# First channel product of a token and channel mixer: four of twelve output tiles of blocks 2 to 5 by seven block products

## The chip, the cores and the metric

One core of one Trainium2 chip. The metric is device time in microseconds (us) of one execution; lower is better. TensorE (PE) does the matmuls and writes PSUM, which has eight banks of 128 partitions x 512 float32. VectorE (DVE) and ScalarE (ACT) work elementwise on SBUF and PSUM, GpSimd (POOL) and SyncE (SP) mostly issue DMAs. Each engine executes its own instructions in the order in which they were issued.

## What is computed

Eight batches of 3008 rows. First a gated attention, then an MLP mixer over tokens and one over channels, each with a residual:

```python
scores = (1.0 / S) * np.matmul(z, z.transpose(0, 2, 1))     # z: 8 x 3008 x 64
attn = np.maximum(scores, 0.0) ** 2
x = u * np.matmul(attn, v)                                  # u, v: 8 x 3008 x 256
...
xt = x.transpose(0, 2, 1)
h = np.maximum(xt @ w_tok1, 0.0) @ w_tok2                   # w_tok1: 3008 x 256
u = x + h.transpose(0, 2, 1)
h2 = np.maximum(u @ w_ch1, 0.0) @ w_ch2                     # w_ch1: 256 x 1536
return u + h2
```

The change concerns `u @ w_ch1` with its ReLU: 256 input channels (two tiles of 128) and 1536 output channels (twelve tiles of 128).

## The kernel before

**Tiles.** A batch's 3008 rows are cut into six blocks of up to 512 rows, q = 0 to 5 (the last has 448). Matmuls are in bfloat16 with float32 sums. PSUM is used as four pairs of two banks (`bank_pair`, L188); a pair is taken by `take_slot` (L940), which picks the one that comes free first, and is returned to the list `ring` with the time at which its reader will be done.

**AV phase.** For each block q the kernel makes scores (`score_run`, L448, line L465), their ReLU on ACT (L503, L491 for the triangle blocks), their square on DVE (L511, L542), and multiplies with v into two accumulators, each a pair of banks (`av_matmul`, L684, line L692; two matmuls of 64 rows run side by side). As the scores are symmetric, a block (q, g) with g > q is also turned by a DMA on SP for later use as (g, q) (`flip`, L558, line L562); it lies in one of the eleven "fl" buffers until then. At a block's end (`finish`, L804) ACT copies one half of an accumulator into a "cp" tile (L820), DVE adds the other half (L826, this frees the pair), and `gate` (L836, lines L846 and L851) multiplies with u into the block's tile `xT`, channels on partitions. This happens for each of the two channel halves, dh = 0 and 1; with dh = 0 the `xT` tile is allocated. "cp" tiles and the transposed `u_sb` tiles of `turn_u2` (L1129, line L1133) share three buffers with the tag "res".

**Mixer work.** It comes in rounds on PE, at the start of a batch's first AV block: first blocks 3 to 5 of the old batch, then the new batch's token mixer (`tok1` L1031, `tok2` L1105, whose result DVE adds to `xT` at L1114), then blocks 0 to 2 of the new batch. A block's channel mixer is:

- six pieces of `ch1` (L1149, line L1162), c2 = 0 to 5. A piece makes two of the twelve output tiles: four matmuls of 512 columns into one bank pair, and one ReLU of 128 x 1024 on ACT (L1201) into the tile `h2pre`.
- four sums of `h2pre` on DVE for each group d of four tiles (`make_sums`, L1227, lines L1241 to L1253) into "hsum", which lies in an "fl" buffer.
- seven products of twelve 128-column matmuls (`product`, L1272, line L1298): the second channel product is already done by seven block products instead of eight, on the sums of `mix_weights`. They go into two pairs, `xb` and `zb`, and DVE collects them (L1334) into "ro", also an "fl" buffer.

The order on PE within a block is written out by hand (end of `add_mixer`): `(0, 0, 1, 2, 0, 6, 5, 0, 7, 3, 0, 4)`, where 1 to 7 are the products of block q and 0 is the next `ch1` piece of block q + 1. So five of the six pieces of block q + 1 are made among the products of block q, and the sixth stands in front of its own products. Block 3's pieces are so made in one round and its products in the next; the sums of its first tiles are put off (`late_sums`) until the end of the AV phase between.

**Planner.** All instructions are placed by host code that keeps a model of the clock: every piece of work has an estimated cost, times at which its inputs will be ready (`Done`), and limits on live buffers (`ROOM`, for example nine `xT`, eleven "fl"). `push` queues an operation for ACT, DVE or SP; the one with the earliest start goes next. Mixer pieces go in the order of their list; AV work goes where no piece is ready. The semaphores for real dependences follow from the tiles.

Of the kernel before, what the change touches and what calls it, by code (L numbers as in the profile page):

```python
# [7 lines left out]

# [5 lines left out]
P = 128  # L14
# [43 lines left out]
def kernel(  # L58
# [42 lines left out]
    w_ch2_sb = consts.tile([P, CHT, D], BF16)  # L101
    w_mix_sb = consts.tile([P, 4, CHT // 2, P], BF16)
    w_sum_sb = consts.tile([P, 3, KT // 2, P], BF16)
    ident = consts.tile([P, P], BF16)

    zs = consts.tile([P, KT + 2, d_qk], BF16)
# [697 lines left out]
    def finish(blk, dh, end):  # L804


        W, acc = blk.W, blk.acc[dh]
        summed = Done()
        guess[blk.home[dh]] = end + 1.7
        ring.append((summed, blk.home[dh]))  # L810

        def load(e):
            return max(free[e], end) + sum(op.busy for op in waiting[e])

        on_act = blk.b > 0 or load("act") + 0.46 < load("dve") + 0.67

        def copy(t):
            cp = sb.tile([P, QW], F32, tag="res", name="cp", bufs=3)
            if on_act:
                nc.scalar.copy(cp[:, :W], acc[:, 1, :W])  # L820
            else:
                nc.vector.tensor_copy(cp[:, :W], acc[:, 1, :W])
            push("dve", t, 0.66, 0.78, lambda t: add(cp, t), first=1, done=summed)

        def add(cp, t):
            nc.vector.tensor_add(cp[:, :W], acc[:, 0, :W], cp[:, :W])  # L826
            push("dve", t, 0.58, 0.7, lambda t: gate(blk, dh, cp, t), first=1,
                 room=(lambda: (blk.b, blk.q) in uTs and has_room(("xT",))) if dh == 0
                 else lambda: (blk.b, blk.q) in xTs)
# [144 lines left out]
    def mix_weights(t):  # L974
# [19 lines left out]

        step(t)

    BORROW = 3
    VERY_LAST = (B - 1, NQ - 1, CHT // 2 - 1)
    ORDER_LAST = ((1, 2, 6, 5, 7, 0, 3, 4), (1, 2, 6, 5, 0, 7, 3, 0, 4))

    def add_mixer(b):
# [97 lines left out]
        def tok2(q, end):  # L1099
            slot, _ = take_slot()  # L1100
            W = widths[q]
            h = bank_pair(slot, "h_ps")
            for dh in range(DT):
                for th in range(2):
                    nc.tensor.matmul(  # L1105
                        h[:, dh, :W], st["a"][:, th, dh * P:(dh + 1) * P],
                        w_tok2_sb[:, th, q * QW:q * QW + W], start=(th == 0), stop=(th == 1))

            def add(t):

                xT = xTs[b, q]
                n = full_tiles[q]
                to = xT[:, :, :n * P].rearrange("p h (t s) -> p h t s", t=n)
                nc.vector.tensor_add(  # L1114
                    to, to, h[:, :, :n * P].rearrange("p h (s t) -> p h t s", t=n))
# [7 lines left out]
                u_done[q].t = t  # L1123
                st["turned", q] = push("sp", t, 1.25, 5.5, lambda t: turn_u2(q, t), first=1,
                                       room=lambda: has_room(("us",)) and (
                                           q <= HALF or goal[0] > (b, 1 + HALF)))
            ring.append((push("dve", end + 0.21, 1.12, 1.25, add, first=2), slot))

        def turn_u2(q, t):  # L1129
            live["us"] += 1  # L1130
            turned_back[b] += 1
            us = sb.tile([P, DT, QW // P, P], BF16, tag="res", name="u_sb", bufs=3)
            nc.sync.dma_start_transpose(  # L1133
                out=us.rearrange("p h t d -> p (h t) d"),
                in_=xTs[b, q].rearrange("p h s -> p (h s)"))
            st["u", q] = us
            release("xT", xT_uses[q])
            for waits in st.pop(("waits", q), []):
                waits(t)

        def with_u(q, ready, fn):

# [6 lines left out]
        def ch1(q, c2, borrowed, end):  # L1149
# [63 lines left out]
                              done=h2_done[q, c2]), slots[0]))  # L1213
            if c2 == CHT // 2 - 1:
                release("xT", xT_uses[q])

        def pairs_of(q):

            return 2 if q < NQ - 1 else 1

        def tiles_of(q, d, r, m):

            n = pairs_of(q)
            return st["h2", q, d].rearrange("p (j r) w -> p j r w", r=2)[
                :, :, r, :2 * n * P].rearrange("p j (i m s) -> p j i m s", m=2, s=P)[:, :, :, m, :]

# [82 lines left out]
        def collect(q, k, end):  # L1309
# [18 lines left out]
            def add(t):  # L1328
                if k == 1:
                    home, n_home = take_home(q)  # L1330
                    st["res", q] = sb.tile([P, QW // P, D], F32, tag=home, name="ro",
                                           bufs=n_home)
                m, h = blocks_of[k]
                nc.vector.tensor_add(  # L1334
                    res(m, h), source, us(m, h) if opening else res(m, h))
                recent[0] = st["res", q][:, 0, :1]
                over[q] -= 1
                if not over[q]:
                    nc.sync.dma_start(
                        out=rows_of(out[b], q)[:, :2 * n, :], in_=st["res", q][:, :2 * n, :])  # L1340
                    free["sp"] = max(free["sp"], t) + 0.4
                    release(home_of(q), [1], t + 4.0)
                    release("us", us_uses[q])

            ready = end + 0.21
            done = taken[q, k]
# [36 lines left out]
        def ch2(q, half, i, end):  # L1383
# [23 lines left out]
            def residual(t):  # L1407
# [28 lines left out]
                        nc.sync.dma_start(out=to, in_=res[r, j, :])  # L1436
                free["sp"] = max(free["sp"], t) + 0.4
                if last:
                    release("us", us_uses[q])
# [11 lines left out]
        def add_ch1(q, c2, by):  # L1451
# [2 lines left out]
                               lambda end: ch1(q, c2, by < q, end),  # L1454
                               room=("h2",) if c2 % 2 == 0 else (),
                               key=(b, 2 + by)))

        def halves(q):

# [43 lines left out]
        for q in range(NQ):  # L1503
            while added[q] < CHT // 2:
                add_next(q, q)
            rest = [(half, i) for half in halves(q) for i in range(pieces_of(q, half))]
            if fast(q):
                us_uses[q][0] += bool(rest)
                h2_uses[q] += bool(rest)
                for k in ORDER_LAST[b % 2] if q == NQ - 1 else (0, 0, 1, 2, 0, 6, 5, 0, 7, 3, 0, 4):  # L1510
                    if k:
# [216 lines left out]
    at_group(NQ * NG + (HALF - 1) * NG + 2,  # L1728
             lambda: push("dve", pe[0], 0.36, 0.5, mix_weights, first=-1))

    def ask_w_tok2(c):
        load_w_tok2(c)
# [189 lines left out]
```

## Time and profile before

| | |
|---|---|
| median of 3 runs | 1113.19 us (1113.01 to 1119.92) |
| profiled execution, first to last instruction (span) | 1110.5 us |
| granted TensorE clock in the profiled execution | 1.000 |
| PE busy | 1105.7 us, 11073 matmuls |
| DVE busy | 782.5 us |
| ACT busy | 669.4 us |
| first channel product (L1162) in the chain that ended last | 22% of the span |
| AV (L692) in that chain | 42% |
| second channel product (L1298) in that chain | 19% (xb 11%, zb 8%) |

The profiled execution's time is known as its span; the runs' times include what lies around it. In a timeline row the columns are start (us from the span's start), duration of the merged group, engine, line, operation, output <- input, shape, count, and in brackets the idle time before it with what ended it. Matmul durations overlap, so the pace of PE is read from start to start. In a row of groups, behind the count: busy us in total, mean ns of one, idle time of the engine before them and what ended it. In a row of windows: from:to, length, then busy time and count of PE, PE's weight loads (PEld), DVE, ACT and POOL, then granted clock, DMA share and GB/s. In a row of waits: who waited for whom, us in total, times, longest. A round of mixer work begins at 198.2, 335.5, 472.2, 607.7, 744.4, 880.0 and 1014.3 us.

### The profile page before, as it was taken

To read this page: it belongs to the slowest core of one execution; us is meant where nothing else is said; L and a number is where in the kernel's file an instruction comes from. 1 tells how busy PE (TensorE), PEld (TensorE's weight loads), DVE (VectorE), ACT (ScalarE), POOL (GpSimd) and SP (SyncE) were. 2 spreads that over 40 slices of the span, in tenths; PEclk is the share of its full clock that TensorE was granted. 3 is DMA by queue.
4 is the path that set the end of the run, shared out by engine and by line. 5 is a ranking of instruction groups with operands and counts; after the bars stand their busy time and mean duration, and the time that the engine had idled before them with its cause. 6 is when DMAs were issued, how large, how long until landed. Compare 5 with 4: busy or idle time off the path is not lost.

```text
span 1110.5 us, 27244 instructions
## 1 busy us (share of the span) xinstructions
PE 1105.7 (100%) x11073; PEld 683.8 (62%) x11073; DVE 782.5 (70%) x1888; ACT 669.4 (60%) x843; POOL 164.3 (15%) x382
## 2 busy tenths in 40 slices
PE   9999999999999999999999999999999999999998
PEld 3444575766557665576556865557655676556676
DVE  6889865975758857588566885578756777556775
ACT  7999555645854567545665456653666536743454
POOL 5320110221003110032100311003210120000100
PEclk9999999999999999999999999999999999999999
DMA  9999947796977969779697797967979678693222
GB/s 177 155 194 164 192 98 143 141 174 134 191 133 141 180 148 174 133 147 203 135 183 119 131 214 139 172 123 152 202 154 170 111 148 182 127 164 93 67 58 96
DMA packets 465725, 165.54 MB, mean 149 GB/s; under 512 B 433024, under 2 KB 448960, under 8 KB 465600
## 3 DMA queue, kind: packets, MB, share of 16 engines
q1 hardware_dynamic: 436208, 131.11, 58.6%
q0 software_dynamic: 28880, 32.32, 21.2%
q8 instruction: 86, 1.41, 0.5%
q10 hardware_dynamic: 512, 0.38, 0.1%
q14 instruction: 39, 0.32, 0.1%
HBM read 65.40 MB, written 24.64 MB: 81 GB/s over the span
## 4 chain that ended last, share of the span: by engine, by line
PE 99%; DMA 1%; issue 0%; POOL 0%; DVE 0%; POOLq 0%
PE acc L692 42%; PE hp L1162 22%; PE xb L1298 11%; PE zb L1298 8%; PE sc L465 6%; PE h_ps L1105 4%; PE a_ps L1031 3%; PE op L1398 2%; PE first_acc L609 1%; DMA v_sb<-in_v_dram 1%; PE zp L184 0%; PE up L1700 0%; DVE res L1433 0%; POOL ident masks.py:199 0%; POOL ident masks.py:197 0%
## 5 line engine op out<-in xcount | busy, mean ns | idle before, releaser
L1201 ACT ACTIVATE h2pre<-hp 128x1024 bf16<-128x1024 f32 (+1 forms) x287 | 278.5, 1008 | 204.0 <-PE hp L1162 171.5
L692 PEld LDWEIGHTS <-v_sb 64*128 64x128 bf16 x4418 | 246.3, 94 | 210.9
L692 PE MATMUL acc<-at,v_sb 64*128 64x512 bf16 (+1 forms) x2738 | 340.9, 375 | 0.0
L503 ACT ACTIVATE at<-sc 128x1024 bf16<-128x1024 f32 (+1 forms) x290 | 286.6, 1027 | 62.5 <-PE sc L465 54.8
L1162 PE MATMUL hp<-xT,w_ch_sb 128*128 128x512 bf16 (+1 forms) x1152 | 274.7, 375 | 0.0
L511 DVE TENSOR_TENSOR at<-at 128x1024 bf16<-128x1024 bf16 (+1 forms) x290 | 198.2, 687 | 103.8 <-ACT at L503 99.9
L692 PE MATMUL acc<-fl,v_sb 64*128 64x512 bf16 (+1 forms) x1680 | 192.5, 367 | 0.0
L1162 PEld LDWEIGHTS <-w_ch_sb 128*128 128x128 bf16 x1152 | 105.6, 98 | 98.1 <-issue 3.0
L1298 PEld LDWEIGHTS <-hsum 128*128 128x128 bf16 x2088 | 124.4, 98 | 18.2 <-issue 0.3
L465 PE MATMUL sc<-zT 64*128 64x512 bf16 (+1 forms) x732 | 131.8, 359 | 0.2 <-ACT zT L1750 0.2
L1298 PEld LDWEIGHTS <-h2pre 128*128 128x128 bf16 x1566 | 95.5, 98 | 20.1
L820 ACT COPY cp<-acc 128x512 f32<-128x512 f32 (+1 forms) x94 | 54.9, 584 | 77.8 <-PE acc L692 66.8
L826 DVE TENSOR_TENSOR cp<-acc,cp 128x512 f32<-128x512 f32 (+1 forms) x94 | 63.5, 676 | 50.7 <-ACT cp L820 50.1
L1241 DVE TENSOR_TENSOR hsum<-h2pre 128x512 bf16<-128x512 bf16 (+1 forms) x141 | 56.1, 402 | 40.7 <-ACT h2pre L1201 39.4
L491 ACT ACTIVATE at<-sc 128x512 bf16<-128x512 f32 (+3 forms) x152 | 56.2, 447 | 41.5 <-PE sc L465 41.0
L1298 PE MATMUL xb<-w_mix_sb,hsum 128*128 128x128 bf16 x1044 | 73.7, 219 | 0.0
L1334 DVE TENSOR_TENSOR ro<-xb,u_sb 128x256 f32<-128x256 f32 (+1 forms) x141 | 56.5, 401 | 22.5 <-PE xb L1298 20.5
L542 DVE TENSOR_TENSOR at<-at 128x512 bf16<-128x512 bf16 (+3 forms) x152 | 41.5, 321 | 38.2 <-ACT at L491 38.2
L465 PEld LDWEIGHTS <-zT 64*128 64x128 bf16 x732 | 42.8, 94 | 41.2 <-issue 3.6
L124 POOL CAST mark<-at 128x1 f32<-128x1 bf16 x24 | 8.2, 342 | 372.5 <-DVE at L511 372.5
L846 DVE TENSOR_TENSOR xT<-cp,uT 128x512 bf16<-128x512 f32 (+1 forms) x94 | 62.5, 665 | 0.9
L1253 DVE TENSOR_TENSOR hsum<-h2pre,hsum 128x512 bf16<-128x512 bf16 (+1 forms) x141 | 56.6, 401 | 2.3
(89 smaller groups left out, 968.4 us busy)
## 6 DMA issues: line engine op xcount, KB each, us to landing
out_dram<-ro SPq DMA_DIRECT2D x40, 512.0 KB, 3.0
v_sb<-in_v_dram POOLq DMA_DIRECT2D x40, 256.0 KB, 4.6
ur<-in_u_dram POOLq DMA_DIRECT2D x40, 256.0 KB, 4.9
w_tok_sb<-in_moe_w_tok_dram POOLq DMA_DIRECT2D x10, 256.0 KB, 10.7
zs<-in_z_dram POOLq DMA_DIRECT2D x35, 64.0 KB, 3.8
at<-at SPq DMA_TRANSPOSE x114, 2.4
out_dram<-ro SPq DMA_DIRECT2D x7, 256.0 KB, 3.5
fl<-at SPq DMA_TRANSPOSE x105, 4.7
```

What stands on the lines that cost most here:

```text
L465: nc.tensor.matmul(sc[:, r, c0:c1], zT[h, k:k + P], zT[h, m + c0:m + c1], start=True, stop=True)
L491: nc.scalar.activation(a3[:, i, c0:c1], sc[:, r, c0:c1], ACT.Relu, scale=inv_S)
L503: nc.scalar.activation(view, sv, ACT.Relu, scale=inv_S)
L511: nc.vector.tensor_mul(view, view, view)
L692: nc.tensor.matmul(o, vs[blk.b, g][rows, i, dh * P:(dh + 1) * P], rhs, start=(dh, h) not in blk.begun, stop=stop, skip_group_check=True)
L826: nc.vector.tensor_add(cp[:, :W], acc[:, 0, :W], cp[:, :W])
L846: nc.vector.tensor_mul(xT[:, dh, :full * P].rearrange("p (t s) -> p t s", s=P), acc[:, :full * P].rearrange("p (t s) -> p t s", s=P), uT[: ...
L1162: nc.tensor.matmul(hps[r % len(hps)][:, r, :W], w_ch1_sb[:, dc, cc * P:(cc + 1) * P], xT[:, dc, :W], start=(dc == 0), stop=(dc == DT - 1))
L1201: nc.scalar.activation(h2[:, :, :W], hp[:, :, :W], ACT.Relu)
L1253: nc.vector.tensor_sub(kind(3), tiles_of(q, d, 1, 0), kind(1))
L1298: nc.tensor.matmul(to[:, i * P:(i + 1) * P], lhs, weights[:, c2, :], start=(first_use and c2 == 0 and i == 0), stop=(c2 == CHT // 2 - 1), ...
L1334: nc.vector.tensor_add(res(m, h), source, us(m, h) if opening else res(m, h))
```

## The change

For batches 1 to 7 and blocks q = 1 to 4 the first four output tiles (d = 0, pieces c2 = 0 and 1) are made in another way: 28 sets. A set is a 2 x 2 block product: the block's tokens are taken as even and odd 128-token tiles, the four output tiles as even and odd, the input channels as two tiles. Instead of eight block products there are seven, each of two matmuls of 256 columns, on sums of the weights (`w_hid_sb`, made once by `hidden_weights`, four operations on DVE) and sums of the tokens (`token_quarters`, T, three operations on DVE: one of 512, two of 256 elements). T and a copy s5 of a partial sum lie in one "fl" buffer. The set works in one bank pair in four stages on PE, and the copying of partial sums goes from bank to bank:

- a: four matmuls; then ACT copies bank 1 to s5 ("keep") and bank 0 into bank 1 ("fork")
- b: four matmuls; then ACT makes the ReLU of bank 1 (512) and copies bank 0 into bank 1 again
- c: four matmuls; then one DVE operation adds s5 to both banks and clamps at zero (1024 elements)
- d: two matmuls; then ACT makes the ReLU of bank 1 (512), and the sums of the group follow

Each stage waits for the operations behind the one before. The order by hand for such blocks is `("a", 0, 1, 2, "b", 6, 5, 0, "c", 7, 3, 0, "d", 4)`. The sums of block 3's first group are no longer put off.

Room for the new weights is made by eight `xT` buffers instead of nine, and the planner now counts the three "res" buffers: the copy of an accumulator and the transposition of u each wait for room.

```diff
-    live = {"at": 0, "fl": 0, "xT": 0, "h2": 0, "us": 0}
-    ROOM = {"at": 6, "fl": 11, "xT": 9, "h2": 6, "us": 2}
+    live = {"at": 0, "fl": 0, "xT": 0, "h2": 0, "us": 0, "res": 0}
+    ROOM = {"at": 6, "fl": 11, "xT": 8, "h2": 6, "us": 2, "res": 3}
...
-        push(engine, end + 0.21, busy, busy + 0.15, copy, first=1)
+        push(engine, end + 0.21, busy, busy + 0.15, copy, first=1, room=("res",))
+
+    def gated_copy(blk, dh, cp, t):
+        gate(blk, dh, cp, t)
+        live["res"] -= 1
...
+            products = [
+                [(0, w1[:, 0, 0], x[0][0], True), (1, w_hid_sb[:, 0], T[:, 0], True)],
+                [(1, w1[:, 0, 1], x[1][0], False), (0, w_hid_sb[:, 1], T[:, 2], False)],
+                [(0, w_hid_sb[:, 3], x[1][1], False), (1, w_hid_sb[:, 2], T[:, 1], False)],
+                [(1, w1[:, 1, 1], T[:, 3], False)]][stage]
+            for r, lhs, rhs, begins in products:
+                for j in range(2):
+                    nc.tensor.matmul(
+                        ps[:, r, j * 2 * P:(j + 1) * 2 * P].rearrange("p (i s) -> p i s", s=P), lhs[:, j, :], rhs,
+                        start=begins and j == 0, stop=True, skip_group_check=True)
...
+            def fork(t):
+                nc.scalar.copy(half(1), half(0))
+
+            def keep(t):
+                nc.scalar.copy(s5, half(1))
+                push("act", t - 0.16, 0.62, 0.78, fork, first=2, done=g_done[q, d, 0])
+
+            def relu_first(t):
+                nc.scalar.activation(h[:, 0, 0], half(1), ACT.Relu)
+                push("act", t - 0.16, 0.62, 0.78, fork, first=2, done=g_done[q, d, 1])
+
+            def relu_last(t):
+                nc.scalar.activation(h[:, 1, 0], half(1), ACT.Relu)
+                recent[0] = h[:, 1, 0, :1]
+                release("fl", [1], t)
+                make_sums(q, d, t)
+
+            def add_two(t):
+                nc.vector._custom_dve(
+                    TENSOR_ADD_SAT, out=h[:, :, 1, :], in0=ps,
+                    in1=s5.unsqueeze(1).to_broadcast([P, 2, QW]), s0=3.0e38, s1=0.0)
```

More of the change, by code (lines that the diff above doesn't have):

```diff
@@ L5 @@
 from concourse import bass_utils, mybir
+from concourse.dve_ops import TENSOR_ADD_SAT
 from concourse._compat import with_exitstack
@@ L817, in copy @@
         def copy(t):
+            live["res"] += 1
             cp = sb.tile([P, QW], F32, tag="res", name="cp", bufs=3)
@@ L826, in add @@
             nc.vector.tensor_add(cp[:, :W], acc[:, 0, :W], cp[:, :W])
-            push("dve", t, 0.58, 0.7, lambda t: gate(blk, dh, cp, t), first=1,
+            push("dve", t, 0.58, 0.7, lambda t: gated_copy(blk, dh, cp, t), first=1,
                  room=(lambda: (blk.b, blk.q) in uTs and has_room(("xT",))) if dh == 0
@@ L1123, in add @@
                 u_done[q].t = t
+                if ("want", q) in st:
+                    st.pop(("want", q))(t)
                 st["turned", q] = push("sp", t, 1.25, 5.5, lambda t: turn_u2(q, t), first=1,
-                                       room=lambda: has_room(("us",)) and (
+                                       room=lambda: has_room(("us", "res")) and (
                                            q <= HALF or goal[0] > (b, 1 + HALF)))
@@ L1130, in turn_u2 @@
             live["us"] += 1
+            live["res"] += 1
             turned_back[b] += 1
@@ L1139, in turn_u2, with release_u @@
                 waits(t)
+        def release_u(q):
+            release("us", us_uses[q])
+            if not us_uses[q][0]:
+                live["res"] -= 1
         def with_u(q, ready, fn):
```

108 lines of the change are left out of this document (104 added, 4 removed).

## Prediction

> **What bounds the kernel now.** I read the page first (busy shares and the chain), then who TensorE (PE) waited for, then the groups, and last the timeline of one round of mixer work with the windows over it.
>
> ```profile
> span 1110.5 us, 27244 instructions
> PE 1105.7 (100%) x11073; PEld 683.8 (62%) x11073; DVE 782.5 (70%) x1888; ACT 669.4 (60%) x843; POOL 164.3 (15%) x382
> PE 99%; DMA 1%; issue 0%; POOL 0%; DVE 0%; POOLq 0%
> PE wp L205 <- DVE zero L1569: 1.2, 1, 1.2
> PE first_acc L609 <- DMA v_sb<-in_v_dram: 0.4, 1, 0.4
> PE sc L465 <- ACT zT L1750: 0.2, 1, 0.2
> ```
>
> The first two lines give span and busy time, the third the chain that ended last, the others are all the waits of PE: 1.8 us in total. The chain is PE for 99%. So a matmul column taken away shortens the span, and any wait put in front of PE lengthens it: no slack on PE absorbs one. The other engines have idle time, 328 us on VectorE (DVE) and 441 us on ScalarE (ACT).
>
> PE's pace comes from start-to-start times, since the durations overlap:
>
> ```profile
> 498.68 1.47 PE L1398 MATMUL op<-w_ch_sb,h2pre 128*128 128x256 bf16 x12
> 499.99 0.50 PE L1298 MATMUL zb<-w_ch_sb,hsum 128*128 128x128 bf16 x6
> ...
> 519.25 0.83 PE L1298 MATMUL xb<-w_mix_sb,h2pre 128*128 128x128 bf16 x12
> 519.51 1.02 ACT L1201 ACTIVATE h2pre<-hp 128x1024 bf16<-128x1024 f32 x1 [1.24 <-PE hp L1162]
> 519.92 2.75 PE L1162 MATMUL hp<-xT,w_ch_sb 128*128 128x512 bf16 x12
> 520.98 2.94 ACT L1201 ACTIVATE h2pre<-hp 128x1024 bf16<-128x1024 f32 x3 [0.45 <-PE hp L1162]
> 522.51 0.83 PE L1298 MATMUL xb<-w_ch_sb,h2pre 128*128 128x128 bf16 x12
> 523.18 0.83 PE L1298 MATMUL zb<-w_ch_sb,h2pre 128*128 128x128 bf16 x12
> ```
>
> Twelve 512-column matmuls take 522.51 - 519.92 = 2.59 us, 0.2158 each; twelve of 256 columns 499.99 - 498.68 = 1.31, 0.109 each; a product of twelve with 128 columns 0.67 in all, 0.056 each. A piece of the first channel product (four matmuls of 512) thus takes 0.863. ACT starts a piece's ReLU 0.26 after the next piece begins on PE (519.25 to 519.51).
>
> **The change part by part.** Durations of what stands beside it:
>
> ```profile
> L1201 ACT ACTIVATE h2pre<-hp 128x1024 bf16<-128x1024 f32 x240 | 237.0, 1025 | 168.2 <-PE hp L1162 147.6 <-issue 12.4 <-DVE hsum L1250 5.9
> L820 ACT COPY cp<-acc 128x512 f32<-128x512 f32 x78 | 46.3, 594 | 53.8 <-PE acc L692 53.8
> L491 ACT ACTIVATE at<-sc 128x512 bf16<-128x512 f32 x38 | 23.0, 605 | 37.4 <-PE sc L465 36.9
> L1114 DVE TENSOR_TENSOR xT<-xT,h_ps 128x1024 bf16<-128x1024 bf16 x40 | 47.5, 1217 | 4.3 <-PE h_ps L1105 3.9
> L1241 DVE TENSOR_TENSOR hsum<-h2pre 128x512 bf16<-128x512 bf16 x120 | 50.1, 422 | 26.5 <-ACT h2pre L1201 26.2
> L921 DVE TENSOR_TENSOR d_pair<-x_pair 128x256 bf16<-128x256 bf16 x96 | 25.5, 289 | 0.1
> L1298 PEld LDWEIGHTS <-hsum 128*128 128x128 bf16 x2088 | 124.4, 98 | 18.2 <-issue 0.3
> ...
> 475.00:490.00 15.00, 15.00 (x188) 11.65 (x186) 15.00 (x57) 8.99 (x10) 6.50 (x14) 1.00 0.86 147
> 510.00:540.00 30.00, 30.00 (x329) 21.23 (x329) 20.13 (x55) 18.82 (x20) 7.01 (x17) 1.00 0.93 184
> ```
>
> *Matmuls.* For batches 1 to 7 and blocks q = 1 to 4 (28 sets), eight matmuls of 512 columns (8 x 0.2158 = 1.726) become fourteen of 256 (14 x 0.109 = 1.526). PE gains 0.20 a set, 28 x 0.20 = **-5.6 us**. That is all that the change can save: 0.5%. The six extra weight loads cost nothing as long as the matmuls hide them; the 128-column products load weights of 98 ns for every matmul and still step at 56 ns.
>
> A rule of the Trainium skill speaks against this (page "TensorE: Matmul & The Clock Gate", section "Back-to-back issue gap"): in a stream of load and matmul pairs the spacing is set by both, about 81 ns at 128 columns and 131 ns at 512. By that, eight to fourteen instructions would lose more than the halved width wins. This trace does not agree, with 56 ns and 216 ns in just such streams, and the measurement decides.
>
> *ACT.* Two ReLUs of 1024 (2 x 1.025) go; one copy PSUM to SBUF (0.594, L820), two copies of one bank into the other, and two ReLUs of 512 (0.605, L491) come. No row shows ACT writing PSUM. The nearest is L820, the same size and source, 0.594; the upper end is 1.025, the row of twice the size; a lower end below 0.594 would change nothing, as will be seen. I take 0.594: 2.99 - 2.05 = +0.94 a set, three sets to a second half of a round (window 510 to 540): 18.8 + 2.8 of 30 us. ACT is no bound by its sum.
>
> The Trainium skill (page "ScalarE: Activation LUTs", section "Step-by-step: what each stage is for") says ScalarE reaches PSUM faster than SBUF; no run here shows it yet, and by it the bank copies would be no longer than L820's row.
>
> *The ACT chain between PE stages.* Stage b waits for the second bank copy, which stands behind the 0.59 "keep" copy and the ReLU of the piece before. Count from the end of that piece: stage a takes 0.44 on PE, then a piece (0.863) and products 1 and 2 (2 x 0.67) stand before b, so PE arrives at 2.64. ACT starts the old ReLU at 0.26, ends it at 1.28, then keep and fork: 1.28 + 0.59 + 0.59 = 2.46, and 0.1 to signal PE makes 2.56. Hidden, by 0.08 us. With 1.025 for the fork it would be 0.35 late, 28 x 0.35 = 10 us. I take 0, range 0 to 10. Stage c has the same 2.2 us of other work before it and only the short ReLU and a fork behind a ReLU already running: about 0.4 to spare.
>
> *DVE.* Three sums for T (0.42 + 2 x 0.29) and the clamped add of 1024 from PSUM: +2.2 a set. The add is a custom operation without a row; L1114 (1.217, two inputs, PSUM, same size) is the nearest, twice that is the upper end. Stage d waits for it: products 7 and 3 and a piece lie between, 2.2 us, against 0.26 + 1.22 + 0.1. Hidden by 0.6; at 2.43 it would cost 28 x 0.6 = 17, which I hold unlikely. Three sets in window 510 to 540 make DVE 20.1 + 6.6 = 26.7 of 30. Window 475 to 490 is already full (15.00 of 15), but there the change also takes out work: the sums of block 3's first four tiles, which were put off to the end of the AV phase and ran into this stretch, are now made in the round before (4 x 0.42 = 1.7 less, 1.2 more). Zero. The weight sums are four operations of about 0.3, once, at low priority: zero, hidden under AV.
>
> *xT from nine buffers to eight.* This is the part that costs. At a round's start nine blocks of xT want to live: blocks 3, 4, 5 of the old batch and 0 to 5 of the new one. With eight, the gate of block 5 (L846) must wait until the last piece of block 3, the first PE work of the round, has read its buffer.
>
> ```profile
> 471.79 1.31 SPq L1133 DMA_TRANSPOSE u_sb<-xT  x1
> 472.22 2.77 PE L1162 MATMUL hp<-xT,w_ch_sb 128*128 128x512 bf16 x12
> 472.37 0.55 DVE L846 TENSOR_TENSOR xT<-cp,uT 128x384 bf16<-128x384 f32 x1
> ...
> 473.15 0.53 ACT L820 COPY cp<-acc 128x448 f32<-128x448 f32 x1 [1.81 <-DVE xT L851]
> 473.58 2.86 ACT L1201 ACTIVATE h2pre<-hp 128x1024 bf16<-128x1024 f32 x3
> 473.72 0.62 DVE L826 TENSOR_TENSOR cp<-acc,cp 128x448 f32<-128x448 f32 x1 [0.65 <-ACT cp L820]
> ...
> 474.82 0.83 PE L1298 MATMUL xb<-w_ch_sb,h2pre 128*128 128x128 bf16 x12
> ACT cp L820 <- DVE xT L851: 11.0, 7, 1.8
> ```
>
> Today the gate runs at 472.37, 0.15 after the round began. Then it can't start before 472.22 + 0.863 + 0.26 = 473.34: 0.97 later. Behind it hangs a chain that is there already (last row: seven times, 11.0 us, hidden so far): the second copy of an accumulator needs a "res" buffer, all three being held by two transposed u and the first copy, which the gate frees; ACT's ReLUs are queued behind this copy; and the add (473.72 to 474.34) frees a bank pair. Shifted by 0.97, the pair is free at 475.31, signalled by about 475.35. In the new order product 1 wants a pair at 472.22 + 0.863 + 0.437 + 0.863 = 474.39 (today at 474.82, so today's slack is 0.4); the other pairs hold stage a and two pieces whose ReLUs stand behind the same copy. PE stalls 0.97, six rounds (batches 1 to 6 as the old batch): **+5.8 us**. The copy's new "res" room orders this wait in the planner but doesn't take it away. Bounds: 0, if a pair is free after all, and 1.5 if product 2 waits as well.
>
> ```profile
> 198.20 4.49 PE L1162 MATMUL hp<-xT,w_ch_sb 128*128 128x512 bf16 x20
> 198.38 0.55 DVE L846 TENSOR_TENSOR xT<-cp,uT 128x384 bf16<-128x384 f32 x1
> ...
> 199.16 0.53 ACT L820 COPY cp<-acc 128x448 f32<-128x448 f32 x1 [0.26 <-DVE xT L851]
> ```
>
> At batch 0's end block 3 has three pieces left, so the gate waits until 198.20 + 3 x 0.863 + 0.26 = 201.05, the copy until 201.83 (0.78 behind, as now), its add ends 1.19 later at 203.02. The fifth piece wants a pair at 201.65: **+1.4**, bounds 0 and 2.7.
>
> *"fl" buffers.* T with its kept copy holds one of eleven; block 4's T and block 3's early sums are held through the whole AV phase, so nine are left for turned attention blocks.
>
> ```profile
> 563.64 7.60 SPq L562 DMA_TRANSPOSE fl<-at  x3
> 563.84 1.92 PE L692 MATMUL acc<-fl,v_sb 64*128 64x512 bf16 x16
> fl<-at SPq DMA_TRANSPOSE x105, 4.7
> ```
>
> Block 2's three turns (563.64) now follow the AV steps that free buffers, one by one, some 2 to 8 us later. They are needed by AV only from about 581 on, 12 us a block, and land 4.7 us after issue: hidden, 0; upper end one late landing a phase, 6 x 4.7 = 28. The SP queue gets no instruction more.
>
> *Sum.* -5.6 + 5.8 + 1.4 + 0 = +1.6. Against the profiled execution's span of 1110.5 that gives 1112.1; the runs' median of 1113.19 lies 2.7 above that span, so **1115** (1114.8).
>
> **The rivals.** *The gain stays*: the planner finds a free pair or the gate's wait hides; 1113.2 - 5.6 = 1107.6. For it: only one buffer decides. Against: the counted nine, and seven waits that exist already. *Slower, the ACT chain*: at a bank copy above 0.67 us stage b waits in every set; at 1.025, +10, 1125, over 1% slower from about 1.0 on. For it: 0.08 of slack, and no row of such a copy. Against: L820 at 0.594. *Slower, AV starves for turned blocks*: 1114.8 + 28 = 1143; against it the 12 us a block. *Weight loads bind*: six loads of 0.098 unhidden, 28 x 0.59 = 16.5, 1131; the 56 ns of the products speak against it, and this is the mechanism of the skill's spacing rule above.
>
> **How the numbers follow.** The gain paid back at the rounds' starts 0.54 (1112 to 1118); gain stays 0.25 (1106 to 1110); ACT chain 0.15 (1119 to 1128); AV starves 0.05; loads bind 0.01. Range 1107 to 1124: it leaves out the last two, part of the chain's case and the best part of the gain's, under 2 in 10. One per cent, 11 us, is about what a measurement of this kernel tells from no change. Faster by that needs twice the whole saving: 0.02. Slower: half the chain's case and the last two, 0.14. The rest, 0.84, within.
>
> **What would show it.** The pace: a set's fourteen matmuls in 1.53 us. The stall: a gap of about 1 us on PE ahead of the first xb product in each round, with L846 waiting for PE; PE's waits would show it for the first time. Bank copies near 0.6 us, the clamped add near 1.2. If PE shows waits for those copies in every set, the chain's rival holds; if no gap stands at the rounds' starts, the first rival.

## The result, and the profile after

| | before | after |
|---|---|---|
| median of 5 runs | 1113.01 us (1112.32 to 1119.92) | 1124.83 us (1121.17 to 1128.2) |
| ratio | | 1.0101, interval 1.0076 to 1.0126 |
| profiled execution's span | 1110.5 us | 1119.3 us (time 1121.17) |
| granted TensorE clock, profiled | 1.000 | 1.000 |
| granted clock, the four other runs | | 0.997 to 0.998 |

The prediction was 1115 (1107 to 1124): the kernel came out 9.8 us slower than that, just outside the range. There are two things to explain: the profiled span grew by 8.8 us where +1.6 was worked out, and the four other runs, with spans of 1123.0 to 1126.4, took another 4 to 7 us, with a clock slightly under full.

In the changed kernel the first channel product stands at L1199, the sets' matmuls at L1323, fork at L1331, keep at L1334, the clamped add at L1348, T's sums at L1278 to L1288, the second channel product at L1448, its collecting add at L1484 and the write of `ro` at L1489. The gate is at L853 and L858, the accumulator's copy at L823 and its add at L829. The head of the page, and its chain that ended last:

```profile
span 1119.3 us, 27630 instructions
PE 1100.0 (98%) x11161; PEld 702.2 (63%) x11241; DVE 831.3 (74%) x2004; ACT 691.0 (62%) x927; POOL 163.0 (15%) x382
PE 93%; DVE 4%; DMA 1%; ACT 1%; issue 1%; ACTq 0%
```

The span is longer, and PE holds only 93% of the chain instead of 99%. DVE has 4% of it. PE's busy time is 5.7 us less than before (1105.7 to 1100.0), but that is no measure of the saved columns: this trace has 80 matmuls fewer than weight loads (11161 and 11241), so records are missing from it, and the run without sets, further down, has a busy time of 1104.1. The saving is read from the pace below. PE now waits, and six rows of the view of waits say for whom (us in total, times, longest):

```profile
ACT cp L823 <- DVE xT L858: 17.8, 7, 2.7
DVE xT L853 <- PE hp L1199: 8.8, 8, 1.3
DVE t_sums L1278 <- DMA out_dram<-ro: 7.4, 4, 2.8
PE xb L1448 <- DVE cp L829: 4.6, 6, 0.8
PE gp L1323 <- DVE h2pre L1348: 3.7, 3, 1.6
PE hp L1199 <- DVE cp L829: 1.1, 1, 1.1
```

The first, second, fourth and sixth lines are one story, the one that was predicted: the gate waits for PE to read the eighth `xT`, the copy waits for the gate, and PE waits for the add that frees a bank pair, six times at a round's start and once at batch 0's end. The third and fifth lines are another, which was not: T's sum waits for the write of `ro`, and stage d for the clamped add.

The new operations take what was assumed for them (mean ns behind the busy time):

```profile
L1348 DVE CUSTOM_DVE_ANT_1 h2pre<-gp,t_sums 128x1024 bf16<-128x1024 f32 x28 | 34.2, 1221 | 7.0 <-PE gp L1323 7.0
L1331 ACT COPY gp<-gp 128x512 f32<-128x512 f32 x56 | 31.9, 570 | 1.8
L1334 ACT COPY t_sums<-gp 128x512 f32<-128x512 f32 x28 | 16.4, 586 | 0.0
```

And the pace of a block with a set, from a stage b to the next block's:

```profile
518.29 0.38 PE L1323 MATMUL gp<-xT,w_ch_sb 128*128 128x256 bf16 x2
527.96 0.38 PE L1323 MATMUL gp<-xT,w_ch_sb 128*128 128x256 bf16 x2
```

That is 9.67 us. The predicted saving of 0.20 us a set would make it that from 9.87, which is what 24 matmuls of 512 and seven products take at the quoted paces (24 x 0.2158 + 7 x 0.67 = 9.87). A block without a set does take 9.87 (rows under "No sets"). So where nothing makes PE wait, a set saves its 0.20 us, 28 times 5.6.

Where the 8.8 us come from, read start to start as in the prediction (time between the starts of two matmuls, less the pace of the first):

| place | times | us |
|---|---|---|
| six round starts, ahead of product 1 | 6 x 0.92 | 5.5 |
| the same rounds, ahead of product 6 | 6 x 0.22 | 1.3 |
| stage d of a set, at 397.32, 533.93 and 672.98 | 1.74 + 0.69 + 1.81 | 4.2 |
| end of batch 0, at 203.76 | 1 | 1.3 |
| single waits at 142.64, 1037.96 and 1105.21 | 0.52 + 0.37 + 0.48 | 1.4 |
| sets | 28 x -0.20 | -5.6 |
| sum | | 8.1 |

0.7 us of the 8.8 stay unassigned. The round's start in the timeline of the changed kernel:

```profile
477.08 0.56 DVE L853 TENSOR_TENSOR xT<-cp,uT 128x384 bf16<-128x384 f32 x1 [1.09 <-PE hp L1199]
477.86 0.53 ACT L823 COPY cp<-acc 128x448 f32<-128x448 f32 x1 [2.73 <-DVE xT L858]
478.43 0.62 DVE L829 TENSOR_TENSOR cp<-acc,cp 128x448 f32<-128x448 f32 x1 [0.45 <-ACT cp L823]
479.10 0.83 PE L1448 MATMUL xb<-w_ch_sb,h2pre 128*128 128x128 bf16 x12 [0.76 <-DVE cp L829]
```

Gate, copy, add, product 1, each waiting for the one above it: the chain of the prediction, link by link. And a stage d that waits:

```profile
373.53 15.47 SPq L564 DMA_TRANSPOSE fl<-at  x5
387.05 0.41 DVE L1484 TENSOR_TENSOR ro<-xb,u_sb 128x256 f32<-128x256 f32 x1
390.45 0.53 SPq L1489 DMA_DIRECT2D out_dram<-ro  x1
395.38 0.42 DVE L1278 TENSOR_TENSOR t_sums<-xT 128x512 bf16<-128x512 bf16 x1 [2.68 <-DMA out_dram<-ro]
396.05 1.22 DVE L1348 CUSTOM_DVE_ANT_1 h2pre<-gp,t_sums 128x1024 bf16<-128x1024 f32 x1
397.32 0.38 PE L1323 MATMUL gp<-t_sums,w_ch_sb 128*128 128x256 bf16 x2 [1.57 <-DVE h2pre L1348]
```

Five turned attention blocks hold SP's queue for 15.5 us, and a transposition of u behind them for another 1.3. The last add into an output tile `ro` ends at 387.46, but its write is issued only at 390.45, behind all these, and the "fl" buffer is free when the write has landed, just before 395.38. That is 7.9 us after the add; the planner counts 4.0 (`release(home_of(q), [1], t + 4.0)`). T of the next block wants that very buffer. Its first sum stands in VectorE's order ahead of the clamped add of the set that is under way, holds VectorE for 2.68 us, and stage d comes late.

### The profile page after: what moved, and what is told of

It is laid out like the page before. It is cut to its first block, busy times and chain, and to the rows that moved or that the text cites. A ratio compares the mean times of both kernels' runs of the same rounds, so it can differ in the third digit from the quotient of the medians.

```text
span 1119.3 us, 27630 instructions
## 1 busy us (share of the span) xinstructions
PE 1100.0 (98%) x11161; PEld 702.2 (63%) x11241; DVE 831.3 (74%) x2004; ACT 691.0 (62%) x927; POOL 163.0 (15%) x382
## 4 chain that ended last, share of the span: by engine, by line
PE 93%; DVE 4%; DMA 1%; ACT 1%; issue 1%; ACTq 0%
PE acc L694 42%; PE hp L1199 15%; PE xb L1448 9%; PE zb L1448 7%; PE sc L467 7%; PE h_ps L1133 4%; PE a_ps L1059 3%; PE gp L1323 3%; PE op L1548 2%; DMA out_dram<-ro 1%; PE first_acc L611 1%; DVE xT L853 1%; DVE ro L1484 1%; ACT h2pre L1238 0%; DVE h2pre L1348 0%
## 5 line engine op out<-in xcount | busy, mean ns | idle before, releaser
L1238 ACT ACTIVATE h2pre<-hp 128x1024 bf16<-128x1024 f32 (+1 forms) x231 | 227.3, 1003 | 180.1 <-PE hp L1199 176.7
L1199 PE MATMUL hp<-xT,w_ch_sb 128*128 128x512 bf16 (+1 forms) x858 | 222.7, 373 | 4.8 <-DVE cp L829 1.1
L694 PE MATMUL acc<-fl,v_sb 64*128 64x512 bf16 (+1 forms) x1680 | 194.9, 367 | 0.0
L1199 PEld LDWEIGHTS <-w_ch_sb 128*128 128x128 bf16 x928 | 85.0, 98 | 73.5 <-issue 4.4
L1448 PEld LDWEIGHTS <-hsum 128*128 128x128 bf16 x2088 | 124.4, 98 | 8.7 <-issue 2.5
L823 ACT COPY cp<-acc 128x512 f32<-128x512 f32 (+1 forms) x94 | 54.9, 584 | 88.4 <-PE acc L694 70.5
L1448 PEld LDWEIGHTS <-h2pre 128*128 128x128 bf16 x1566 | 95.5, 98 | 20.0 <-issue 6.3
L829 DVE TENSOR_TENSOR cp<-acc,cp 128x512 f32<-128x512 f32 (+1 forms) x94 | 63.4, 675 | 57.4 <-ACT cp L823 57.2
L1448 PE MATMUL xb<-w_mix_sb,hsum 128*128 128x128 bf16 x1044 | 73.8, 219 | 1.2 <-DVE ro L1484 0.5
L1484 DVE TENSOR_TENSOR ro<-xb,u_sb 128x256 f32<-128x256 f32 (+1 forms) x141 | 56.2, 399 | 18.1 <-PE xb L1448 17.5
L853 DVE TENSOR_TENSOR xT<-cp,uT 128x512 bf16<-128x512 f32 (+1 forms) x94 | 62.2, 663 | 9.5 <-PE hp L1199 8.8
```

What stands on the lines that cost most here:

```text
L694: nc.tensor.matmul(o, vs[blk.b, g][rows, i, dh * P:(dh + 1) * P], rhs, start=(dh, h) not in blk.begun, stop=stop, skip_group_check=True)
L853: nc.vector.tensor_mul(xT[:, dh, :full * P].rearrange("p (t s) -> p t s", s=P), acc[:, :full * P].rearrange("p (t s) -> p t s", s=P), uT[: ...
L1199: nc.tensor.matmul(hps[r % len(hps)][:, r, :W], w_ch1_sb[:, dc, cc * P:(cc + 1) * P], xT[:, dc, :W], start=(dc == 0), stop=(dc == DT - 1))
L1238: nc.scalar.activation(h2[:, :, :W], hp[:, :, :W], ACT.Relu)
L1448: nc.tensor.matmul(to[:, i * P:(i + 1) * P], lhs, weights[:, c2, :], start=(first_use and c2 == 0 and i == 0), stop=(c2 == CHT // 2 - 1), ...
L1484: nc.vector.tensor_add(res(m, h), source, us(m, h) if opening else res(m, h))
```

## The experiments

Theory A: what the kernel pays is two waits, the gate of block 5 (eight `xT` buffers) and T's first sum behind the write of `ro`. Theory B, the rival, changes with the question: first that the sets and their sums on VectorE cause the waits at the round starts too; later that there are too few "fl" buffers, so that a wait taken from one place only turns up at another.

### No sets

```diff
-            return b > 0 and 0 < q <= HALF + 1 and d == 0
+            return False
```

> The changed kernel without a single set: all first products are made as before, but xT has eight buffers, the res buffers are counted and the weight sums are made. Theory A (the loss comes from the eight xT buffers): with the old order product 1 wants its bank pair 0.4 us later than in the changed kernel, so each of six round starts stalls about 0.5 us and the first one about 1.3: span 1110.5 + 6 x 0.5 + 1.3 + 0.5 = 1115. Rival B (the sets' own ACT and DVE work costs the time): span 1110.5, as before, and no waits of PE.

Measured: 1119.31 us, ratio 1.0062 (1.0043 to 1.0081), span 1116.5. Three of its waits, and product 1 of two blocks in a row:

```profile
ACT cp L823 <- DVE xT L858: 17.8, 7, 2.7
PE xb L1448 <- DVE cp L829: 2.0, 6, 0.3
PE hp L1199 <- DVE cp L829: 1.1, 1, 1.1
525.51 0.83 PE L1448 MATMUL xb<-w_ch_sb,h2pre 128*128 128x128 bf16 x12
535.38 0.83 PE L1448 MATMUL xb<-w_ch_sb,h2pre 128*128 128x128 bf16 x12
```

The copy's wait of 17.8 us is exactly that of the changed kernel, without a single set. Start to start PE loses 6 x 0.50 ahead of product 1, 5 x 0.28 ahead of product 6, 1.31 at batch 0's end and 0.52 at 142.01: 6.2 us, against a span 6.0 longer. So the change without its sets costs 6 us, in waits behind the gate of block 5 (A); B falls. That this is the eighth `xT` alone is argued from where the waits stand: the run also counts the "res" buffers and makes the sums of the weights. With the sets the wait at a round's start is 0.92 instead of 0.50: stage a is 0.43 us shorter than a piece, so product 1 arrives 0.42 sooner at a pair that is free no earlier.

### The last piece of block 3 made early

```diff
-                for k in (ORDER_LAST[b % 2] if q == NQ - 1 else GROUPED if grouped(q + 1) else
+                for k in (ORDER_LAST[b % 2] if q == NQ - 1 else
+                          GROUPED + (0,) * (q == HALF - 1) if grouped(q + 1) else
```

> The changed kernel with block 3's sixth piece moved from the start of the next round to the end of the round that makes the other five, so that the oldest xT is free long before the gate of block 5 wants it. Theory A: the six gaps of 0.92 us ahead of product 1 and the 0.22 us ahead of product 6 behind them go, 6.8 us; the one at 203.8 (batch 0 keeps its three late pieces) and the three stage-d waits stay: span 1119.3 - 6.8 = 1112.5. Rival B: the span stays at 1119.

Measured: 1118.36 us, 1.0048 (1.0034 to 1.0062), span 1116.3. Two of the waits of PE that are left:

```profile
PE gp L1323 <- DVE h2pre L1348: 6.4, 3, 2.6
PE hp L1199 <- DVE cp L829: 1.1, 1, 1.1
```

The six waits of 0.92 are gone, as A said: with no piece of the old batch left, the eighth buffer is free when the gate comes. Two waits of 0.20 and 0.17 us remain in most of these rounds. But the span fell by 3.0 only, 3.8 short of what was expected, since the three at stage d grew from 4.2 to 6.9 us (2.81, 1.72, 2.40): PE came sooner to a buffer that the write of `ro` frees no sooner.

### The output tile's buffer counted free later

```diff
-                    release(home_of(q), [1], t + 4.0)
+                    release(home_of(q), [1], t + 8.0)
```

The planner is told nearly what the trace shows (7.9 us), once for the changed kernel and once with the early piece.

> The changed kernel, where the planner counts the output tile's fl buffer as free 8 us after its last collect instead of 4 (its DMA waits behind five turned blocks on the SP queue). Theory A: T's first sum no longer sits on VectorE waiting for that DMA in front of the clamped add, the three stage-d waits of 1.74, 0.69 and 1.81 us go: span 1119.3 - 4.2 = 1115. Rival D (VectorE is simply full there and the DMA wait only shows it): no change, 1119.

> Both edits together. Theory A: span 1119.3 - 6.8 - 4.2 = 1108.3, below the kernel before by 2 us, the rest of the 5.5 us being held back by 1.3 us at batch 0's end and 1.4 us of other waits. Rival B: above 1115. On the clock: if the long gaps of PE bring the lower granted clock (0.997 to 0.998 in four of five runs of the changed kernel), all runs of this kernel show 1.000 and the median lies about 2 us above the span; if the sets themselves do, they show 0.998.

Measured: 1129.05 us, 1.0146 (1.0124 to 1.0167), span 1127.9; with the early piece 1121.3 us, 1.0076 (1.006 to 1.0093), span 1118.8. Both spans miss what was expected, by 13 and 10 us. The waits at stage d did go; others came. Two that the run with both edits has:

```profile
ACT a_sb L1110 <- DVE a_f L1090: 23.1, 7, 3.6
PE h_ps L1133 <- ACT a_sb L1110: 7.0, 7, 1.7
```

The token mixer's `a_f` takes an "fl" buffer as well. With the later release the planner thought it later, and put another VectorE operation, which itself waits for PE, ahead of its sums:

```profile
503.46 0.42 DVE L1583 TENSOR_TENSOR res<-op,u_sb 128x256 f32<-128x256 f32 x1 [0.96 <-PE op L1548]
503.80 0.28 DVE L1484 TENSOR_TENSOR ro<-zb,ro 128x128 f32<-128x128 f32 x1
504.00 0.41 DVE L1075 TENSOR_TENSOR a_f<-a_ps,a_f 128x256 f32<-128x256 f32 x1
```

In the run with the early piece alone that sum ran at 502.64, 0.27 us behind the copy it needs (502.10 + 0.27). So a truer number in the planner made a worse order: it delays every user of the pool, not only T. Without the early piece, two single waits of 2.05 and 1.55 us at 107.08 and 1045.07 came on top, whose cause stays open. If the waits at stage d bring the lower clock, all runs with both edits should have shown 1.000; five of six did, and one had 0.998.

### The output tile written on another queue

Here the plan stays the same to the last instruction; only the queue of one DMA changes. The changed kernel itself ran beside it, as base.

```diff
-                    nc.sync.dma_start(
+                    nc.gpsimd.dma_start(
```

> The changed kernel once more, as the base of the runs beside it. If its time is a property of the program, the profiled span is again near 1119.3 us and the median between 1121 and 1125 (ratio 1.008 to 1.010). If the runs without a profile were high by accident the first time, the median comes nearer to 1121.

> The changed kernel with one edit: the output tile ro is written out on GpSimd's queue instead of SyncE's, in the same place of the plan. Theory A (T's first sum on VectorE waits for ro's buffer, and ro's write waits on SyncE's queue behind five turned attention blocks): the three waits of PE at stage d (1.74, 0.69 and 1.81 us) are gone, span 1119.3 - 4.2 = 1115.1. Theory B (there are simply too few fl buffers at that moment, whatever queue writes ro): the waits stay, span 1119.3. Both expect the 0.92 us at the six round starts to stay. GpSimd's loads of v stand behind the new DMA; if they came late, PE would show waits for v_sb.

Measured: the changed kernel again 1125.25 us, 1.0119 (1.0104 to 1.0134), span 1121.2; with the write on GpSimd's queue 1125.72 us, 1.0123 (1.0109 to 1.0136), span 1127.3. Two of the three waits went (397 and 673), the one at 532 stayed with 0.45 us, and a new one of 7.26 us came at 950.46. It shows the mechanism better than the others:

```profile
922.56 14.38 SPq L564 DMA_TRANSPOSE fl<-at  x4
937.02 1.32 SPq L267 DMA_TRANSPOSE uT<-ur  x1
940.45 0.53 POOL L257 DMA_DIRECT2D ur<-in_u_dram  x1 [11.19 <-DMA uT<-ur]
940.98 0.54 POOL L1489 DMA_DIRECT2D out_dram<-ro  x1
948.52 0.42 DVE L1278 TENSOR_TENSOR t_sums<-xT 128x512 bf16<-128x512 bf16 x1 [8.20 <-DMA out_dram<-ro]
950.46 0.59 PE L1323 MATMUL gp<-t_sums,w_ch_sb 128*128 128x256 bf16 x2 [7.10 <-DVE h2pre L1348]
```

On GpSimd's queue the write stands behind a load of u, which waits 11.19 us for a transposition, which stands on SP behind four turned blocks. The same blocks delay the write by way of two queues, and T's sum waits 8.20 us for it. The chain of theory A holds; the cure doesn't. During the long wait the clock falls, and it stands at half for 10.24 us (945.59 to 955.83).

The base run shows the second thing that was to be explained. Windows around the wait at stage d (the third figure from the end is the granted clock), two of the changed kernel's second trace, then two of the run with the early piece alone:

```profile
394.23:397.64 3.41, 1.55 (x14) 0.82 (x11) 2.57 (x6) 1.27 (x2) 0.42 (x1) 1.00 0.85 173
397.64:401.05 3.41, 3.19 (x17) 2.00 (x16) 2.82 (x9) 1.18 (x2) 0.00 (x0) 0.50 0.32 117
392.47:395.88 3.41, 2.19 (x28) 1.56 (x26) 0.48 (x2) 1.63 (x2) 0.71 (x2) 1.00 1.25 129
395.88:399.29 3.41, 1.94 (x19) 1.36 (x20) 3.41 (x9) 0.60 (x1) 0.00 (x0) 1.00 0.59 116
```

In the base run PE had waited 1.85 us until 396.98, and then ran at half its clock from 397.64 to 401.05, which costs about 1.7: that run has a clock of 0.998 and a span 1.9 longer than the first. A longer wait at the same place, 2.6 us until 397.30, did nothing in the run with the early piece.

The bounds of these windows are those of the clock itself. In the four traces that have half a clock in mid-run (this one, the write on GpSimd's queue, and the two runs of the next section) the clock falls a whole number of steps of 3.413 us after its first rise at the program's start: 115 steps here (5.11 to 397.64), 275, 277 and 276 in the others. Cut into such steps, the thirteen traces with a record of the clock show a fall behind a step in which PE was busy for 1.55 us or less (1.55 here, 1.19, 0.73 and 0.00 in the others; the remaining traces have their only fall at the program's end), and none where it was busy for 1.67 or more. The wait of 1.85 us lies in one step; the wait of 2.6 is split between two, which have 2.19 and 1.94 us of work. So the place of a wait counts as much as its length, and that place changes from run to run: the first rise stands at 4.0 to 7.2 us in these traces.

The Trainium skill (page "TensorE: Matmul & The Clock Gate", section "What's actually happening") says that the clock falls to half after an idle window of about 3.4 us, and that the window runs freely. The half clock and the free-running steps agree with these traces; that a whole window must be idle does not, as PE was busy for 1.55 us of the one before the fall.

### Both together, and batch 0 too

The early piece with the write on GpSimd's queue, and then all pieces of block 3 early in batch 0 as well:

```diff
-    BORROW = 3
+    BORROW = 6
...
-                          (0, 0, 1, 2, 0, 6, 5, 0, 7, 3, 0, 4)):
+                          (0, 0, 1, 2, 0, 6, 5, 0, 7, 3, 0, 4) + (0,) * (q == HALF - 1)):
```

> The early last piece of block 3 (no wait at the round starts) together with the write of ro on GpSimd's queue. Theory A: the waits at stage d of the run with the early piece alone (2.81 + 1.72 + 2.40 = 6.9 us) go, span 1116.3 - 6.9 = 1109.4, time about 1111.4, some 1 us under the kernel before. Theory B: they stay, span 1116.3, time 1118.4.

> The run with both, and all six pieces of block 3 of batch 0 made early too. Theory: the 1.31 us wait at the end of batch 0 goes as the six others did, span 1.3 under that of the run with both (1108.1 if that is 1109.4; time about 1110.1). Rival: the three pieces made early are only moved to where batch 0's start needs their bank pairs or h2pre buffers; then another wait takes its place, and the span is the same or longer.

Measured: 1124.86 us, 1.011 (1.0097 to 1.0124), span 1124.6; and 1123.9 us, 1.0106 (1.0078 to 1.0134), span 1121.5. Both spans miss what was expected, by 15 and 13 us, through waits of the same kind. The two longest lines of the first:

```profile
PE xb L1448 <- DVE ro L1484: 4.8, 5, 2.1
PE gp L1323 <- DVE h2pre L1348: 3.8, 1, 3.8
```

The second line is again the late write on GpSimd; in the first, VectorE's sums of the sixth block wait for the same write (2.64 us at 629.99) and hold up the collecting adds; the first also has a single wait of 3.0 us for a turned block at 102.52. The second has both kinds too, 5.4 and 5.0 us. With the write on GpSimd's queue all fourteen runs of the three kernels have a clock of 0.995 to 0.998. One expectation was met: in the second run the wait of 1.31 us at batch 0's end is gone and none took its place there.

### T behind the clamped add

SP keeps the write, no buffer comes free sooner. T is asked for one piece later, so that its first sum stands behind the clamped add; stage a waits for this sum only, and the other two may come after.

```diff
-            if c2 == (3 if q else 0) and q + 1 < NQ and grouped(q + 1):
+            if c2 == (4 if q else 0) and q + 1 < NQ and grouped(q + 1):
...
-                push("dve", t - 0.1, 0.27, 0.4, third)
+                push("dve", t - 0.1, 0.27, 0.4, third, first=-1)
...
-                push("dve", t - 0.1, 0.27, 0.4, fourth, done=t_done[q])
+                push("dve", t - 0.1, 0.27, 0.4, fourth, first=-1)
...
-                push("dve", t, 0.4, 0.53, first_two, room=("fl",), frees=fl_free)
+                push("dve", t, 0.4, 0.53, first_two, room=("fl",), frees=fl_free, done=t_done[q])
```

It ran alone, with the early piece, and with that and batch 0's pieces:

> The changed kernel with T asked for one piece later (after the fifth piece of the block before instead of the fourth), stage a waiting for T's first sum only, and the two other sums with low priority. ro is still written on SyncE's queue and no fl buffer comes free earlier; only VectorE's order changes, so that the clamped add no longer stands behind T's first sum. Theory A: the waits of 1.7, 0.7 and 1.8 us at stage d are gone, span 1119.3 - 4.2 = 1115.1, plus at most 13 waits of 0.2 us that the later T may bring (2.5). And if the lower granted clock (0.997 to 0.998) of the changed kernel's runs comes from those waits, as one of its traces shows for the wait at 396.98, all runs now show 1.000 and the median lies 2.0 above the span, near 1117. Theory B (the fl buffers as such are the bound): the wait moves to stage a of the next block, span 1119 or more.

> The later T together with the early last piece of block 3. Theory A: span 1116.3 - 6.9 = 1109.4, plus at most 2.5 for the later T; granted clock 1.000 in all runs; time 1111.4 to 1114. Theory B: span 1116 or more.

> The same, and all six pieces of block 3 of batch 0 made early. In the run with the write on GpSimd's queue this took the wait of 1.31 us at batch 0's end away; here span 1.3 under that of the run with the later T and the early piece, near 1108 to 1110.6, time 1110 to 1112.6: 0 to 2.5 under the kernel before. If the buffers as such are the bound: 1115 or more.

Measured: alone 1119.12 us, 1.0055 (1.0034 to 1.0076), span 1117.7; with the early piece 1114.26 us, 1.0011 (0.9999 to 1.0023), span 1112.4; with batch 0 too 1113.59 us, 1.0006 (0.9989 to 1.0023), span 1111.8. The spans are 0.1 to 1.2 us over the upper ends that were expected. The same moment in the first of them:

```profile
390.89 0.53 SPq L1489 DMA_DIRECT2D out_dram<-ro  x1
394.25 1.23 DVE L1348 CUSTOM_DVE_ANT_1 h2pre<-gp,t_sums 128x1024 bf16<-128x1024 f32 x1 [1.00 <-PE gp L1323]
396.13 0.38 PE L1323 MATMUL gp<-t_sums,w_ch_sb 128*128 128x256 bf16 x2
396.81 0.43 DVE L1391 TENSOR_TENSOR hsum<-h2pre 128x512 bf16<-128x512 bf16 x1 [0.67 <-DMA out_dram<-ro]
397.16 0.42 DVE L1278 TENSOR_TENSOR t_sums<-xT 128x512 bf16<-128x512 bf16 x1
```

The write is as late as ever (390.89), VectorE still meets it, for 0.67 us at 396.81. But the clamped add stands in front and waits for PE alone, and stage d (396.13) for nothing. Order was what cost, not the number of buffers: B falls here too. All six runs have a clock of 1.000, as have all twelve with the early piece, where all the runs without a profile of the changed kernel itself had 0.997 to 0.998. The early piece alone, whose waits at stage d are longer, had 0.998 in four of six runs; the two kernels with the later release, which don't have them, 1.000 in eight of ten. That the waits at stage d cost those runs their clock is so supported by one trace and by these runs. They are not its only cause: one of six runs without sets, two of twelve of the kernel with batch 0's pieces, and one of 23 runs of the kernel before beside them had 0.998 as well.

The later T has its price: fourteen waits of about 0.13 us inside product 6, which the order of the change didn't have. A start-up wait of about 1 us for a DMA (the load of v in the first two of these traces, one for z in the third), which the changed kernel's trace doesn't have, comes on top. Some of what PE still waits for in the run with the early piece:

```profile
PE hp L1199 <- DVE cp L829: 1.1, 1, 1.1
PE first_acc L611 <- DMA v_sb<-in_v_dram: 0.9, 1, 0.9
PE xb L1448 <- DVE hsum L1396: 0.6, 2, 0.4
```

### The repaired order without the sets

The same early pieces with `grouped` returning False, the last run.

> No sets, eight xT buffers, all six pieces of block 3 early in every batch: what the repaired order of the rounds is worth without the block products. Theory A: the six waits of 0.50 and the one of 1.31 us of the run without sets go, of its waits of 0.28 at most the five stay, and about a microsecond at other places: span 1116.5 - 3.0 - 1.3 = 1112.2 or a little less, time 1112 to 1114.5. Beside it the run with sets, later T and early pieces (span 1111.8, time 1113.59) then shows what the sets are worth on the chip once the larger waits are gone: next to nothing of their 5.6 us, since T's sums and the clamped add on VectorE cost PE about as much in small waits. Rival: the sets' gain arrives in full and what is left over is the cost of eight xT; then this run takes 1117 to 1119.

Measured: 1114.68 us, 1.0016 (1.0007 to 1.0025), span 1113.3. Beside the last kernel with sets (1113.59, 1.0006, 0.9989 to 1.0023) the sets are worth 1.1 us of their 5.6, and the intervals overlap. The time is 0.2 us over what was expected, and the rival (1117 to 1119) falls. Even the 1.1 is not shown to be the sets' own: this run has two single waits, 0.99 us at 353.79 and 0.76 at 899.16, that the other hasn't. No version was faster than the kernel before; the two nearest can't be told from it.

Not tried: the sets with nine `xT` (the change gave up the ninth to make room for its weights); the kernel before with eight `xT` and nothing else.

## Why the prediction was wrong, point by point

- *Matmuls, -5.6*: right. The period of a block with a set is 9.67 us, and 9.87 without. The weight loads cost nothing, so the spacing rule of the Trainium skill (page "TensorE: Matmul & The Clock Gate", section "Back-to-back issue gap"), the rival with 16.5 us, did not come true here.
- *ACT chain, 0 with 10 as its end*: right. The bank copy takes 0.570 us, not the 0.594 taken; no stage waited for it. That rival is refuted.
- *DVE, 0 for the durations*: the clamped add takes 1.221 us (1.217 assumed). The margin of 0.6 us that was worked out is real, and it is what was overdrawn: by a wait ahead of the add on VectorE, not by its length.
- *xT, +5.8 and +1.4*: the mechanism right link by link, the size too: 6 x 0.92 = 5.5 and 1.3. What was missing is the echo in the same rounds, 6 x 0.22 = 1.3, since VectorE, shifted by the late gate, collects product 1 late as well.
- *"fl" buffers, "hidden, 0"*: this is the step that failed. It asked what T takes from the turned attention blocks in the AV phase, and not what T itself has to wait for. Its buffer is the one that `ro` has just given up, and the write of `ro` stands on SP behind those blocks. "The SP queue gets no instruction more" was true and beside the point: there is a new waiter for an old one. The upper end of 28 us stood for another mechanism (AV starving), of which the changed kernel's trace shows nothing; the one wait of AV for a turned block, 3.0 us with the write on GpSimd's queue, stands in batch 0, which has no sets. Measured: 4.2 us in the profiled execution, and VectorE's order is the link that carried it, as the later T showed. By itself this would have made 1119; the echo, the single waits and the clock took the time past the upper end.
- *The offset of 2.7 us between span and median*: it took the clock as given. The changed kernel's own offset was 1.9 in its profiled execution (1121.17 - 1119.3), and the spans of its other runs lay 4 to 7 us higher, with less clock. One stretch of 3.41 us at half takes about 0.0015 off the mean clock of such a span (an estimate from the figures above), so 0.998 is one stretch and 0.997 two: 1.7 to 3.4 of those 4 to 7 us. The rest stays open. Such waits were not in the profile of before (1.8 us in all, at the start), so nothing in it had a price for them.

In sum: -5.6 + 5.5 + 1.3 were predicted and came; +1.3 (echo), +4.2 (T) and 1.4 (single waits) were not, and 0.7 of the 8.8 us between the spans is unassigned. Between the medians lie 11.8 us: the median run's clock of 0.998 stands for some 1.7 more, and about 1.3 stay open.

## What to carry to other kernels

When a change adds a user to a pool of buffers, ask first what the new user waits for: who gives the buffer up, on which queue its last transfer stands, and behind what. Then ask what stands behind the new instruction in the order of its own engine; an instruction that is off the critical path holds up everything that follows it. Where PE was 99% of the chain, one new wait a round (5.5 us) took back all of half a per cent of saved work (5.6 us).

## What the runs showed of the hardware

A copy from one PSUM bank to another by ScalarE takes 570 ns for 128 x 512 float32, less than the 586 ns into SBUF. The Trainium skill (page "ScalarE: Activation LUTs", section "Step-by-step: what each stage is for") says that ScalarE reaches PSUM faster than SBUF; the trace agrees, by 16 ns. A custom add and clamp of 1024 elements from PSUM takes 1221 ns, as much as an ordinary add of that size from PSUM (1217). And the granted clock can fall to 0.50 for 3.41 us after a wait of 1.85 us on TensorE, so that such a wait costs about as much again; it fell behind steps of 3.41 us with 1.55 us of work or less and behind none with 1.67 or more, so that a wait of 2.6 us split between two steps cost no clock.
